# Gated linear attention and an SSM block on one core: blocks of 32 steps with a carried state, computed in small tiles of the TensorE array

## The chip, the core and the metric

The program runs on one core of a Trainium2 chip. A core has TensorE (a 128 x 128 multiply array that reads SBUF and writes PSUM), VectorE, ScalarE and GpSimd, each with its own in-order stream of instructions, and SyncE, which here only issues DMAs. The engines meet through semaphores. The metric is the device time of one execution in microseconds (us); lower is better. In the profile PE is TensorE's matmul side and PEld its weight loads, DVE is VectorE, ACT is ScalarE, POOL is GpSimd, SP is SyncE.

## The reference

Four batch entries, eight heads, 768 steps, 48 channels a head, all in float32. First a gated linear attention, a recurrence over the steps:

```python
for t in range(S):
    state = alpha[:, :, t, :, None] * state + einsum('bhd,bhe->bhde', k[:, :, t], v[:, :, t])
    y[:, :, t] = einsum('bhd,bhde->bhe', q[:, :, t], state)
```

The heads are then put side by side, x of shape (4, 768, 384), and go through a gated SSM block:

```python
val, gate = split(x @ w_in)              # 512 and 512 features
h = a * h + val[:, t]; ys[:, t] = h      # for each step, a = exp(A_log)
out = (silu(gate) * ys) @ w_out          # back to 384
```

## The kernel before

The sequence of a batch entry is cut into groups of G = 2 chunks of C = 128 steps, so there are 12 groups, three to a batch entry. A group goes through two routines: `attention(n)`, then `ssm(n)`. Both are Python generators; the loop at the end of the kernel runs them turn by turn, so that the pieces of `ssm(n-1)` stand between the levels of `attention(n)`. The tile framework under the kernel then sets the semaphores, and moves an instruction ahead of others of its engine where its own model of the times says so; the lists of instructions below are the order that results.

`attention(n)`, lines 167 to 285. Heads go in pairs, a pair filling the 128 partitions as 2 x 64 channels (48 and 16 of padding).

- Lines 178 to 188 transpose alpha, q and k to channels by steps on PE (`tp`, one PSUM buffer, `ps_tp`) and copy them to `T`, `Q` and `K`.
- Inside a chunk the pairs of steps s < t are dealt with by a binary tree of seven levels, l = 1 to 64. At each level ACT copies the odd blocks of `Q` into `Qz`, block-diagonal by the two heads of a pair (line 207, twice a level); PE computes the scores `sc` of a level with eight matmuls of 128 x 128 by 128 columns (line 218; line 215 for l = 32 and 64, where only the blocks are computed); DVE copies those that belong to the level into `A` through a mask (line 228; ACT at line 225 for l of 16 and more); and the running products grow by one doubling, `Q` on DVE (236), `K` and the block products `T` on POOL (237, 240). The next level's scores need the grown `Q` and `K`.
- For each of the two chunks: the output `y` from `A` and the values (252) and, behind the first chunk, from `Q` and the state `S_bd` (256); then the state of the next chunk, from a transpose of `K` (264), its copy `Kn` (266), the product `s1` with the values (270), the decay (276, 277) and two copies that make it block-diagonal (280).

`ssm(n)`, lines 287 to 323: transposes of x (292), the projection `pj` (302), the scan over the steps on DVE (305), the sigmoid on ACT and two products (310 to 312), the output product `o` (318) and its store. `w_in` and `w_out` come as float64 bits and are converted by eight DVE instructions for each of ten pieces (lines 110 to 121), during the first group.

In the profile a float32 matmul is two records, each a weight load on PEld and a matmul on PE, while a transpose is one: line 218's 480 matmuls are x960. "Record" below means one such pair.

Of the kernel before, what the change touches and what calls it, by code (L numbers as in the profile page):

```python
# [9 lines left out]
FP32 = mybir.dt.float32  # L10
# [7 lines left out]
def kernel(  # L18
# [10 lines left out]
):  # L29
    """Gated linear attention in chunks of C steps, then the gated SSM block, all in float32.  # L30

    Inside a chunk the pair (s < t) is weighted by prod(alpha[s+1..t]) per key channel.  The pairs
    are split by a binary tree: at level l, t lies in an odd block of l steps and s in the even
    block before it, so that the weight is (product from the block's start to t) times (product
    from s to its block's end).  Both are running products of alpha alone, grown level by level
    with the block totals: no logarithm, no division, nothing that overflows by the split.  After
    the last level they are the factors that join the chunk to the state that is carried.
    """
    nc = tc.nc
    B, H, S, D = q.shape  # L40
    DM = H * D                    # 384
    DI = moe_A_log.shape[0]       # 512
    C = 128                       # steps of a chunk
    G = 2                         # chunks of a group
    GC = G * C                    # tokens of a group
    NG = S // GC                  # groups of a batch entry
    NP = H // 2                   # pairs of heads; a pair fills the partitions as 2 x 64
# [4 lines left out]
    LEVELS = [1, 2, 4, 8, 16, 32, 64]  # L52
    ON_ACT = (16, 32, 64)         # blocks that start on partition quadrants: plain copies
    BY_BLOCK = (32, 64)           # products of the blocks alone
# [7 lines left out]
    p3 = pool("p3", 3)  # L62
    wst = pool("wst", 2)
    ps_sc = pool("ps_sc", 2, space=PS)
    ps_tp = pool("ps_tp", 1, space=PS)
    ps_mm = pool("ps_mm", 3, space=PS)

# [1 line left out]
    NBUF = 3  # L69
    pads = [{n: const.tile([C, G, H, DP], FP32, name=f"{n}_pad{i}") for n in "qka"} for i in range(NBUF)]  # L70
# [3 lines left out]
    vs = {}  # L74

    def load(n):
        b, g = divmod(n, NG)
        t = pads[n % NBUF]
        vs[n] = p3.tile([C, G, H, D], FP32, name="v_sb")
        for c in range(G):  # L80
            rows = ds(g * GC + c * C, C)
            for dst, src in ((t["a"][:, c, :, 0:D], alpha), (t["q"][:, c, :, 0:D], q),
                             (t["k"][:, c, :, 0:D], k), (vs[n][:, c], v)):
                nc.sync.dma_start(out=dst, in_=src[b, :, rows, :].rearrange("h p d -> p h d"))

    load(0)
    load(1)

# [6 lines left out]
    nc.sync.dma_start(out=a_log, in_=moe_A_log.rearrange("(a p) -> p a", p=C))  # L95
    nc.scalar.activation(a_dec, a_log, AF.Exp)

    # The weights come as the bits of float64, low word first: to float32, rounded to nearest.
# [3 lines left out]
    def load_weight(dst, src):  # L102
# [6 lines left out]
        # sign and exponent: the float32 +-2^e, with zero and infinity beyond its range  # L109
# [6 lines left out]
        # mantissa: 21 bits of the high word and the low word as their fraction  # L116
# [7 lines left out]
    def load_weights():  # L124
        for kk in range(NK):
            for i in range(2):
                load_weight(w_in[:, kk, ds(i * DI, DI)], moe_w_in[ds(kk * C, C), ds(i * DI, DI)])
                yield
        for cc in range(NI):
            load_weight(w_out[:, cc, :], moe_w_out[ds(cc * C, C), :])  # L130
            yield

    # at level l, column (r, j) of an odd block r takes the rows s of the even block r
    masks = {}
    for l in LEVELS:
        if l in ON_ACT:
            continue
        nb = C // (2 * l)
        mf = p2.tile([C, nb, l], FP32, tag="mask_f", name="mask_f")
        nc.gpsimd.memset(mf, 1.0)  # L140
        nc.gpsimd.affine_select(out=mf, in_=mf, compare_op=ALU.is_ge, fill=0.0, base=0,
                                channel_multiplier=1, pattern=[[-2 * l, nb], [0, l]])
        nc.gpsimd.affine_select(out=mf, in_=mf, compare_op=ALU.is_ge, fill=0.0, base=l - 1,
                                channel_multiplier=-1, pattern=[[2 * l, nb], [0, l]])
        m = const.tile([C, 2 * GP, C // 2], U8, name=f"mask{l}")
        nc.vector.tensor_copy(out=m, in_=mf.rearrange("p b l -> p (b l)")[:, None, :]
                              .to_broadcast([C, 2 * GP, C // 2]))
        masks[l] = m

    # weights of the pairs (s, t): [s, chunk, head, t]; s >= t stays zero  # L150
    As = [const.tile([C, G, H, C], FP32, name=f"A{i}") for i in range(2)]
    # the odd blocks of Q for the products, block-diagonal by the heads of a pair
    Qzs = [const.tile([C, GP, 2, C // 2], FP32, name=f"Qz{i}") for i in range(3)]
    for t in As + Qzs:
        nc.gpsimd.memset(t, 0.0)
    n_qz = 0
    # the state by pairs of heads, block-diagonal
    S_bds = [const.tile([C, NP, 2, D], FP32, name=f"S_bd{i}") for i in range(2)]
    for t in S_bds:
        nc.gpsimd.memset(t, 0.0)  # L160
    S_f = const.tile([C, NP, D], FP32, name="S_f")

    prev_h = [None] * NI

    xs = {}

    def attention(n):
        nonlocal n_qz
        b, g = divmod(n, NG)
        pad, v_sb = pads[n % NBUF], vs.pop(n)  # L170
        A = As[n % 2]

        # channels to the partitions: aT, qT * aT, kT as [(head of pair, channel), chunk, pair, step]
        T = p3.tile([C, 2 * GP * C], FP32, name="T")
        Q = p3.tile([C, G, NP, C], FP32, name="Q")
        K = p3.tile([C, G, NP, C], FP32, name="K")
        aT = T[:, 0:GP * C].rearrange("p (g j t) -> p g j t", g=G, j=NP)
        for name in "aqk":
            for c in range(G):
# [5 lines left out]
                elif name == "q":  # L185
                    nc.vector.tensor_mul(Q[:, c], tp, aT[:, c])  # L186
                else:
                    nc.scalar.activation(K[:, c], tp, AF.Copy)  # L188

        # the pairs s == t, whose weight is one  # L190
        qk = p2.tile([C, G, H, D], FP32, name="qk")
        dg = p2.tile([C, G, H], FP32, name="dg")
        nc.gpsimd.tensor_mul(qk, pad["q"][:, :, :, 0:D], pad["k"][:, :, :, 0:D])
        nc.vector.tensor_reduce(out=dg, in_=qk, axis=mybir.AxisListType.X, op=ALU.add)
        nc.gpsimd.tensor_mul(qk, v_sb, dg[:, :, :, None].to_broadcast([C, G, H, D]))

        # the pairs s < t, level by level
# [48 lines left out]
        for c in range(G):  # L246
# [13 lines left out]
            if last:  # L260
                continue
# [101 lines left out]
```

## Time and profile before

| | |
|---|---|
| median of 2 runs | 668.98 us (667.76 to 670.2) |
| span of the profiled execution, first to last instruction | 655.2 us |
| so, between the span and the runs' times | 12.6 to 15.0 us, 13.8 to the median |
| instructions recorded | 9150 |
| mean granted TensorE clock | 0.893 |
| DMA traffic | 28.91 MB, mean 44 GB/s |

The profile gives no time for its own execution other than the span; what lies around the span is taken as the 13.8 us to the median. Busy times of engines overlap, and a busy PE is not a full array: the records say that a matmul is in flight. The line of the granted clock, in tenths, tells how fast the array was allowed to run. A number in brackets behind a row of the timeline is how long the engine stood idle before it, and what ended that.

### The profile page before, as it was taken

The page shows a single profiled execution, that of the slowest core. Times are in us where ns is not written, and L with a number is a line of the kernel's source. Part 1 is how long each engine was busy: PE and PEld are TensorE (multiplying, and loading weights), DVE is VectorE, ACT ScalarE, POOL GpSimd, SP SyncE. Part 2 cuts the span into 40 slices and gives each one's busy share as a digit, 9 for nine tenths or more (in the row PEclk, how much of TensorE's full clock was granted, in tenths as well). Part 3 has the DMA queues.
Part 4 walks back from the last instruction along what each step waited for, and adds up shares of the span by engine and source line. Part 5 has one row for each costly group of instructions (what it writes and reads, how often), then busy time and mean ns, then how long its engine had stood idle before and what let it go on. Part 6 is the DMA issues. An engine that isn't in the chain of part 4 may idle for free.

```text
span 655.2 us, 9150 instructions
## 1 busy us (share of the span) xinstructions
PE 526.7 (80%) x3608; PEld 440.1 (67%) x3608; DVE 297.1 (45%) x392; ACT 235.5 (36%) x419; POOL 255.5 (39%) x330
## 2 busy tenths in 40 slices
PE   2657159969979978978968968968968968978987
PEld 1546149758768758758757758758758757867775
DVE  4676976138138138127227227226327326315512
ACT  1351034344334334334334334325325325315411
POOL 9732643253243253253343253352342352322411
PEclk9995559979979979979979979988989988987999
DMA  9935520050040050040040040032010000000000
GB/s 158 205 60 124 149 52 2 25 98 0 25 98 1 25 97 2 25 92 5 25 93 5 25 81 16 14 73 36 13 37 1 14 12 2 13 13 1 1 26 25
DMA packets 105307, 28.91 MB, mean 44 GB/s; under 512 B 100912, under 2 KB 103984, under 8 KB 105264
## 3 DMA queue, kind: packets, MB, share of 16 engines
q1 hardware_dynamic: 105264, 28.32, 21.9%
q8 instruction: 29, 0.48, 0.3%
q14 instruction: 14, 0.11, 0.1%
HBM read 23.60 MB, written 4.72 MB: 43 GB/s over the span
## 4 chain that ended last, share of the span: by engine, by line
PE 62%; POOL 11%; issue 10%; ACT 8%; DVE 7%; DMA 1%; POOLq 0%; DVEq 0%; SPq 0%; ACTq 0%
PE sc L218 17%; PE pj L302 11%; PE o L318 10%; POOL K L237 7%; PE y L252 7%; PE tp L182 6%; PE sc L215 5%; ACT Qz L207 3%; DVE Q L186 2%; PE y L256 2%; PE s L270 2%; ACT Kn L266 2%; PE tpk L264 2%; ACT K L188 1%; ACT T L184 1%
## 5 line engine op out<-in xcount | busy, mean ns | idle before, releaser
L218 PE MATMUL sc<-Qz,K 128*128 128x128 f32 x960 | 142.5, 308 | 26.4 <-POOL K L237 25.8
L237 POOL TENSOR_TENSOR K<-K,T 128x512 f32<-128x512 f32 x84 | 99.1, 1180 | 160.0 <-PE sc L218 91.6
L218 PEld LDWEIGHTS sc<-Qz,K 128*128 128x128 f32 x960 | 135.9, 222 | 35.8 <-POOL K L237 33.8
L207 ACT ACTIVATE Qz<-Q 64x512 f32<-64x512 f32 x168 | 107.3, 639 | 136.1 <-DVE Q L186 71.8
L302 PE MATMUL pj<-xT,w_in 128*128 128x256 f32 x576 | 132.3, 381 | 0.6 <-ACT xT L293 0.6
L302 PEld LDWEIGHTS pj<-xT,w_in 128*128 128x128 f32 x576 | 106.5, 191 | 13.3 <-ACT xT L293 0.8
L228 DVE COPY_PREDICATED A<-mask,sc 128x1024 f32<-128x1024 uint8 x48 | 89.6, 1867 | 31.1 <-PE sc L218 30.9
L236 DVE TENSOR_TENSOR Q<-Q,T 128x512 f32<-128x512 f32 x84 | 70.3, 837 | 54.0 <-ACT Qz L207 52.6
L312 POOL TENSOR_TENSOR f<-sg,hh 128x256 f32<-128x256 f32 x48 | 35.0, 730 | 107.6 <-DVE sg L311 98.9
L258 DVE TENSOR_TENSOR x_sb<-y,qk 128x384 f32<-128x384 f32 x24 | 13.4, 557 | 131.3 <-PE y L256 105.6
L318 PE MATMUL o<-w_out,f 128*128 128x384 f32 x192 | 69.2, 504 | 0.6 <-POOL f L312 0.6
L225 ACT ACTIVATE A<-sc 16x256 f32<-16x256 f32 (+2 forms) x84 | 44.1, 525 | 25.1 <-PE sc L215 18.1
L318 PEld LDWEIGHTS o<-w_out,f 128*128 128x128 f32 x192 | 33.7, 189 | 25.1 <-POOL f L312 6.0
L182 PE MATMUL tp<-ident,k_pad 128*128 128x128 f32 x96 | 26.8, 435 | 29.3 <-DVE Q L186 18.5
L252 PEld LDWEIGHTS y<-v_sb,A 128*128 128x128 f32 x384 | 47.8, 200 | 3.6
L182 PE MATMUL tp<-ident,q_pad 128*128 128x128 f32 x96 | 23.9, 392 | 32.3 <-issue 13.4
L280 POOL COPY S_bd<-S_f 64x192 f32<-64x192 f32 x40 | 19.1, 477 | 76.4 <-DVE S_f L277 58.5
L252 PE MATMUL y<-v_sb,A 128*128 128x48 f32 x384 | 48.7, 282 | 0.0
L310 ACT ACTIVATE sg<-pj 128x256 f32<-128x256 f32 x48 | 18.4, 383 | 77.1 <-DVE hh L305 76.9
L240 POOL TENSOR_TENSOR T<-T 128x512 f32<-128x512 f32 (+6 forms) x84 | 36.9, 440 | 19.6 <-ACT T L184 14.3
L182 PEld LDWEIGHTS tp<-ident,k_pad 128*128 128x128 f32 x96 | 17.2, 217 | 38.7 <-DVE Q L186 23.2
L182 PEld LDWEIGHTS tp<-ident,q_pad 128*128 128x128 f32 x96 | 15.0, 193 | 39.3 <-DVE Q L186 14.2
(57 smaller groups left out, 490.9 us busy)
## 6 DMA issues: line engine op xcount, KB each, us to landing
a_pad<-in_alpha_dram SPq DMA_DIRECT2D x24, 192.0 KB, 3.8
q_pad<-in_q_dram SPq DMA_DIRECT2D x24, 192.0 KB, 3.8
k_pad<-in_k_dram SPq DMA_DIRECT2D x24, 192.0 KB, 3.1
v_sb<-in_v_dram SPq DMA_DIRECT2D x24, 192.0 KB, 3.5
out_dram<-o_sb SPq DMA_DIRECT2D x24, 192.0 KB, 1.9
bits<-in_moe_w_in_dram SPq DMA_DIRECT2D x6, 512.0 KB, 5.2
bits<-in_moe_w_out_dram SPq DMA_DIRECT2D x4, 384.0 KB, 3.0
a_log<-in_moe_A_log_dram SPq DMA_DIRECT2D x1, 2.0 KB, 4.3
```

Of the source, the lines that this page charges most:

```text
L182: nc.tensor.transpose(tp[:, j, :], pad[name][:, c, 2 * j:2 * j + 2, :], ident)
L207: nc.scalar.activation(Qz[r, :, i, :].rearrange("p x (b l) -> p x b l", l=l), Qv[r, :, 1, :].rearrange("p (x b) l -> p x b l", b=nb), AF.Copy)
L218: nc.tensor.matmul(sc[:, c, j], K[:, c, j, :], Qz[:, c * NP + j], start=True, stop=True)
L225: nc.scalar.activation(A_b[ds(s0, l), :, ds(s0 + l, l)], sc_b[ds(s0, l), :, ds(r * l, l)], AF.Copy)
L228: nc.vector.copy_predicated(out=A.rearrange("p g h (b two l) -> p (g h b) two l", two=2, l=l)[:, :, 1, :], mask=masks[l].rearrange("p a (b ...
L236: nc.vector.tensor_mul(Qv[:, :, 1, :], Qv[:, :, 1, :], Tv[:, :, 0:1].to_broadcast([C, n2, l]))
L237: nc.gpsimd.tensor_mul(Kv[:, :, 0, :], Kv[:, :, 0, :], Tv[:, :, 1:2].to_broadcast([C, n2, l]))
L240: nc.gpsimd.tensor_mul(Tn, Tv[:, :, 0], Tv[:, :, 1])
L252: nc.tensor.matmul(y[:, h, :], A[:, c, h, :], v_sb[:, c, h, :], start=(h == 0), stop=(first and h == H - 1), skip_group_check=True)
L302: nc.tensor.matmul(pj[:, i, :], w_in[:, kk, ds(i * DI + cc * C, C)], xT[:, kk, :], start=(kk == 0), stop=(kk == NK - 1))
L312: nc.gpsimd.tensor_mul(f[:, cc, :], sg, hh)
L318: nc.tensor.matmul(o, f[:, cc, ds(c * C, C)], w_out[:, cc, :], start=(cc == 0), stop=(cc == NI - 1))
```

## The change

The tree stops at blocks of R = 32 steps: five levels, l = 1 to 16. A state is carried from block to block, eight blocks to a group, instead of from chunk to chunk. Every product of the attention is cut to small tiles of the array, each with its own rows (the channels of one head of the pair, or 32 of the steps) and its own 32 columns:

- scores: per level 64 matmuls of 64 rows by 32 columns, 16 columns moving, straight from strided views of `Q` (no `Qz`, no copies on ACT); the two heads go to two PSUM banks;
- states: `K` is transposed in 32 x 32 squares by one DVE instruction (`Kt`), then 128 matmuls of 32 by 32, 48 moving, in four pieces of 32 (`z`); the carried state `S_n` grows block by block, a product on POOL and a sum on DVE for each of eight blocks;
- outputs: 64 matmuls of 32 by 32 from `A` and the values, 64 of 64 by 32 from `Q` and the states.

`v` is loaded a second time in another layout, `v4`, by 16 DMAs a group. `A` shrinks from 2048 to 512 elements a partition. The masks are made on POOL alone. `attention` is split into four generators and a fixed loop interleaves `levels(n)`, `states(n-1)`, `transposes(n+1)`, `ssm(n-2)` and `outputs(n-1)`: three groups in flight, two more turns of the loop than groups. The scores have one PSUM buffer of two banks instead of two; the input pads have two buffers instead of three. `w_in` is converted value half first.

The diff's core, with the comments that it drops left out:

```diff
-    LEVELS = [1, 2, 4, 8, 16, 32, 64]
+    LEVELS = [1, 2, 4, 8, 16]
...
-    ps_sc = pool("ps_sc", 2, space=PS)
+    ps_sc = pool("ps_sc", 1, space=PS)
     ps_tp = pool("ps_tp", 1, space=PS)
-    ps_mm = pool("ps_mm", 3, space=PS)
+    ps_y = pool("ps_y", 1, space=PS)
+    ps_z = pool("ps_z", 1, space=PS)
+    ps_mm = pool("ps_mm", 2, space=PS)
...
+        v4s[n] = p3.tile([C, GR, NP, D], FP32, name="v4")
+        vv = v[b].rearrange("(j i) s d -> i j s d", i=2)
+        for qd in range(4):
+            for j in range(NP):
+                nc.sync.dma_start(
+                    out=v4s[n][ds(R * qd, R), :, j, :],
+                    in_=vv[qd // 2, j, ds(g * GC, GC), :].rearrange("(r s) d -> s r d", s=R))
...
+    def make_masks():
+        for l in LEVELS:
+            nb = R // (2 * l)
+            mf = p2.tile([C, NR, nb, l], FP32, tag="mask_f", name="mask_f")
+            nc.gpsimd.memset(mf, 1.0)
+            for qd in range(NR):
+                sl = mf[:, qd]
+                nc.gpsimd.affine_select(out=sl, in_=sl, compare_op=ALU.is_ge, fill=0.0, base=-R * qd,
+                                        channel_multiplier=1, pattern=[[-2 * l, nb], [0, l]])
+                nc.gpsimd.affine_select(out=sl, in_=sl, compare_op=ALU.is_ge, fill=0.0, base=R * qd + l - 1,
+                                        channel_multiplier=-1, pattern=[[2 * l, nb], [0, l]])
...
+    def levels(n):
...
+            sc = ps_sc.tile([C, 2, 512], FP32, tag="sc", name="sc")
+            scv = sc[:, :, 0:GP * R // 2].rearrange("p i (x b l) -> p i x b l", x=GP, l=l)
+            for c in range(G):
+                for j in range(NP):
+                    for r in range(NR):
+                        for i in range(2):
+                            rows, steps = ds(DP * i, DP), ds(R * r, R)
+                            nc.tensor.matmul(scv[steps, i, c * NP + j], K[rows, c, j, steps],
+                                             Qr[rows, c, j, r, :, 1, :], start=True, stop=True,
+                                             skip_group_check=True)
...
+    def states(n):
...
+        nc.vector.transpose(out=Kt.rearrange("p x d -> p (x d)"), in_=K.rearrange("p g j t -> p (g j t)"))
...
+            for r in (r2, r2 + 1):
+                g, rr = divmod(r, NR)
+                for j in range(NP):
+                    for qd in range(4):
+                        rows = ds(R * qd, R)
+                        nc.tensor.matmul(zv[rows, r - r2, j, :], Kt[rows, (g * NP + j) * NR + rr, :],
+                                         v4[rows, r, j, :], start=True, stop=True, skip_group_check=True)
...
+                    nc.gpsimd.tensor_mul(dS, S_n[:, r], Tb[:, g, :, rr:rr + 1].to_broadcast([C, NP, D]))
+                    nc.vector.tensor_add(dst, dS, zv[:, r - r2])
...
+    for n in range(N + 2):
+        if n + 2 < N:
+            load(n + 2)
+        if n + 1 < N:
+            load_v(n + 1)
...
+        for p in range(5):
+            step(lv)
+            if n == 0:
+                step(weights)
+                step(weights)
+            if p < 4:
+                step(sa)
+            step(tr)
+            if p < 4:
+                step(sm)
```

The order of PE, in a turn in the middle of the program. Before, one level of scores (eight matmuls) stands between two pieces of the projection, and the transposes of the next group follow in one stretch at the end; `x8` is eight matmuls.

```order
L218 MATMUL sc<-Qz_151,K 128x128 x8
L302 MATMUL pj<-xT,w_in 128x256 x6
L215 MATMUL sc<-Qz_149,K 32x2x32 x16
L318 MATMUL o<-w_out,f 128x384 x4
L215 MATMUL sc<-Qz_150,K 64x128 x8
L318 MATMUL o<-w_out,f 128x384 x4
L252 MATMUL y<-v_sb,A_148 128x48 x8
L256 MATMUL y<-S_bd_157,Q 128x96 x4
L264 MATMUL tpk<-ident,K 128x128 x4
L270 MATMUL s_778<-v_sb,Kn 64x48 x8
```

Here the outputs and the state of one chunk follow each other, before those of the second.

Now, the last two of the five steps of a turn and what follows them (`z` are the states, `tpx` the transposes of x):

```order
L226 MATMUL sc<-Q,K 32x16 x64
L274 MATMUL z<-v_797,Kt 32x48 x32
L195 MATMUL tp<-ident,q_pad_86 128x128 x4
L339 MATMUL pj<-xT,w_in 128x256 x6
L226 MATMUL sc<-Q,K 32x16 x64
L195 MATMUL tp<-ident,k_pad_87 128x128 x4
L299 MATMUL y<-v_sb,A_106 32x48 x64
L309 MATMUL y<-S_n,Q 32x48 x64
L195 MATMUL tp<-ident,k_pad_87 128x128 x4
L355 MATMUL o<-w_out,f 128x384 x4
L324 MATMUL tpx<-ident,x_sb 128x128 x3
L355 MATMUL o<-w_out,f 128x384 x4
```

The transposes, which stood together, are now spread singly between other work. A level's scores are 64 small matmuls in place of 8, a group's states 128 in place of 16 and 8 transposes, its outputs 128 in place of 24.

The order of DVE at the start, where the weights are converted. Before, the first piece follows the growth of the first group's `Q`:

```order
L228 COPY_PREDICATED A_147<-mask_145,sc 128x128x8
L236 TENSOR_TENSOR Q<-Q,T 128x32x16
L236 TENSOR_TENSOR Q<-Q,T 128x16x32
L110 TENSOR_SCALAR ex<-bits 128x512
L117 TENSOR_SCALAR w_in<-bits 128x512
```

Only the doubling for l = 64 is left of the first group's levels when the conversion begins.

Now it follows four levels of the third group:

```order
L243 COPY_PREDICATED A_106<-mask_177,sc 128x64x4
L235 TENSOR_TENSOR Q<-Q,T 128x64x8
L243 COPY_PREDICATED A_106<-mask_192,sc 128x32x8
L284 TENSOR_TENSOR S_n<-dS,z 128x192 x2
L126 TENSOR_SCALAR ex<-bits 128x512
L133 TENSOR_SCALAR w_in<-bits 128x512
```

The conversion moved behind two whole groups of levels on DVE, and the last of the third group's levels stands behind all ten pieces.

264 lines of the change are left out of this document (141 added, 123 removed).

## The prediction

> **What bounds the kernel now.** I read the page first (busy shares, slices, the chain), then the middle of the program in order of time, then the busy times by stretch, then the groups by line.
>
> ```profile
> PE 526.7 (80%) x3608; PEld 440.1 (67%) x3608; DVE 297.1 (45%) x392; ACT 235.5 (36%) x419; POOL 255.5 (39%) x330
> PEclk9995559979979979979979979988989988987999
> PE 62%; POOL 11%; issue 10%; ACT 8%; DVE 7%; DMA 1%; POOLq 0%; DVEq 0%; SPq 0%; ACTq 0%
> ```
>
> PE is the bound, and no other engine is above half; but the chain is PE for only 62%, and the granted clock dips once a group. One group in the middle shows where:
>
> ```profile
> 314.13 2.76 PE L302 MATMUL pj<-xT,w_in 128*128 128x256 f32 x12
> 316.82 1.09 PE L215 MATMUL sc<-Qz,K 128*32 128x64 f32 x32
> 317.84 2.94 PE L318 MATMUL o<-w_out,f 128*128 128x384 f32 x8
> 320.70 1.96 PE L215 MATMUL sc<-Qz,K 128*64 128x128 f32 x16
> 325.28 1.88 PE L252 MATMUL y<-v_sb,A 128*128 128x48 f32 x16
> 329.21 0.67 PE L270 MATMUL s<-v_sb,Kn 128*64 128x48 f32 x16 [0.69 <-ACT Kn L266]
> 333.81 0.66 PE L182 MATMUL tp<-ident,a_pad 128*128 128x128 f32 x4 [0.69 <-ACT T L184]
> 337.09 1.12 PE L182 MATMUL tp<-ident,q_pad 128*128 128x128 f32 x4 [1.27 <-DVE Q L186]
> 344.67 0.49 PE L292 MATMUL tpx<-ident,x_sb 128*128 128x128 f32 x3
> ...
> 0.00:57.90 57.90, 31.21 (x208) 27.25 (x208) 38.60 (x51) 17.70 (x29) 33.25 (x52) 0.93 0.93 139
> 57.90:135.90 78.00, 51.72 (x339) 43.09 (x339) 43.90 (x80) 21.50 (x38) 34.27 (x32) 0.72 0.23 60
> 184.00:234.30 50.30, 42.97 (x302) 35.79 (x302) 21.56 (x27) 19.58 (x35) 20.30 (x25) 0.90 0.17 37
> 584.80:635.00 50.20, 43.15 (x292) 36.08 (x292) 20.06 (x24) 19.37 (x35) 15.17 (x22) 0.90 0.03 9
> 635.00:655.20 20.20, 16.06 (x64) 12.02 (x64) 4.69 (x8) 2.51 (x6) 2.89 (x4) 0.98 0.06 20
> ```
>
> Projection and scores are back to back; from 329 on the transposes wait for their one PSUM buffer, and the same four take 0.66 us and then 1.12, because the clock has been lowered. The last rows are stretches (length; busy PE, PEld, DVE, ACT, POOL; clock; DMA share; GB/s). They cut the program into a start of 135.9 us, nine groups of (584.8 - 135.9) / 9 = 49.9, and an end of 70.4. In a group PE is busy for 43 and waits for 7.
>
> **The small matmuls: the price on which all hangs.** Removed a group are the large products (the last row, a copy of the transposes, is for the turn below):
>
> ```profile
> L218 PE MATMUL sc<-Qz,K 128*128 128x128 f32 x960 | 142.5, 308 | 26.4 <-POOL K L237 25.8
> L215 PE MATMUL sc<-Qz,K 128*64 128x128 f32 x192 | 23.5, 276 | 2.0 <-ACT Qz L207 2.0
> L215 PE MATMUL sc<-Qz,K 128*32 128x64 f32 x384 | 13.1, 221 | 1.6 <-POOL K L237 1.6
> L252 PE MATMUL y<-v_sb,A 128*128 128x48 f32 x384 | 48.7, 282 | 0.0
> L256 PE MATMUL y<-S_bd,Q 128*128 128x96 f32 x160 | 22.1, 283 | 1.9 <-POOL S_bd L280 1.9
> L270 PE MATMUL s<-v_sb,Kn 128*64 128x48 f32 x320 | 14.3, 235 | 12.4 <-ACT Kn L266 12.4
> L264 PE MATMUL tpk<-ident,K 128*128 128x128 f32 x80 | 13.9, 284 | 1.5 <-POOL K L237 1.5
> L184 ACT ACTIVATE T<-tp 128x512 f32<-128x512 f32 x24 | 14.3, 597 | 38.4 <-PE tp L182 38.4
> ```
>
> That is (142.5 + 23.5 + 13.1 + 48.7 + 22.1 + 14.3 + 13.9) / 12 = 23.2 us a group. In their place come 320 + 128 + 128 = 576 small matmuls, 1152 records. At s ns from one record to the next they cost 1.152 s us a group, and are no cheaper than what they replace from s = 20.1 on.
>
> No row has a tile of 64 or 32 rows, so s is bounded from both sides. Above: L215's 32-column form. The median record lasts 220 ns, so (1090 - 220) / 31 = 28 ns lie from one to the next, with 64 columns moving. Its 64-column form takes (1960 - 272) / 15 = 113 ns with 128 moving, 0.88 ns a column, so 64 columns last 56 ns: two records, in two column tiles, must run at once. Below: by the same 0.88 ns, 48 columns in four tiles at once give 10.6 ns and 16 columns in eight give 1.8; weights of 32 columns, at L252's (1880 - 282) / 15 = 107 ns for 128, last 27 ns, in four to eight tiles 3 to 7. So the array alone would allow about 7. Between stands what the sequencer can issue:
>
> ```profile
> L215 PE MATMUL sc<-Qz,K x576: 218/220/324, 42.2 to 622.7; 128*32 128x64 f32 x132, 128*64 128x128 f32 x60
> L182 PEldq EVENT_SEMAPHORE  x2: 51/51/51, 282.7 to 282.8; - x2
> ```
>
> The second row is two waits of PE's own sequencer, 125 ns apart unrounded; the first holds it for 51. Between them in the program stand four transposes, eight instructions. So eight go through in 74 ns, 9.3 each, and a record (load and matmul) in 18.6. It is the nearest row to a long stream of small instructions, and in a turn of this kernel 2304 of them come: I take s = 18.6, and keep 7 and 28 as ends.
>
> [...]
>
> **A turn of the new loop on PE.** Small matmuls 1.152 x 18.6 = 21.4 us. Kept work at full clock: transposes 6 x 0.66 = 4.0, `tpx` 2 x 0.49 = 1.0, projection 4 x 2.6 = 10.4 (its 2.76 less the overlap with the next row), output product 2 x 2.85 = 5.7. Sum 42.5. A change between large and small tiles costs 0.1: L215 begins 2.69 us after the projection ahead of it, which takes 2.6; some 22 changes a turn are 2.2. What else it waits for is hidden by the new order: the transposes now stand singly, with 3 to 6 us of other work between two that share the buffer, against 0.6 for its copy. Left over, two round trips of 0.69: 1.3. Turn: 46.0 us, against 49.9. So PE has nearly as much to do as before; what goes is 7 us of waits and slowed transposes, and what comes is tile changes.
>
> **The engines beside it.**
>
> ```profile
> L207 ACT ACTIVATE Qz<-Q 64x512 f32<-64x512 f32 x168 | 107.3, 639 | 136.1 <-DVE Q L186 71.8 <-DVE Q L236 55.1 <-PE sc L218 5.4
> L237 POOL TENSOR_TENSOR K<-K,T 128x512 f32<-128x512 f32 x84 | 99.1, 1180 | 160.0 <-PE sc L218 91.6 <-PE sc L215 59.1 <-ACT Qz L207 9.3
> L228 DVE COPY_PREDICATED A<-mask,sc 128x1024 f32<-128x1024 uint8 x48 | 89.6, 1867 | 31.1 <-PE sc L218 30.9
> L276 POOL TENSOR_TENSOR S_f<-S_f,T 128x192 f32<-128x192 f32 x16 | 14.1, 881 | 1.3
> L277 DVE TENSOR_TENSOR S_f<-S_f,s 128x192 f32<-128x192 f32 x16 | 5.7, 354 | 17.7 <-PE s L270 17.7
> GB/s 158 205 60 124 149 52 2 25 98 0 25 98 1 25 97 2 25 92 5 25 93 5 25 81 16 14 73 36 13 37 1 14 12 2 13 13 1 1 26 25
> ```
>
> ACT loses line 207 (8.9 us a group) and the copies of `A` and `Kn`: off the path, nothing gained directly. POOL: five `K` products for seven, -2.4, but eight decays of 0.88 for one or two, +5.7: about 22 of 46, hidden. DVE: masked copies of 256 for 1024 elements, five at 0.35 (row 277) to 0.47 (a quarter of 1867) for four, -5; two doublings less; eight sums of 0.35, +2.5; the 32 x 32 transpose of `Kt` is in no row, by the nearest of 1024 elements 0.35 to 1.9: about 19 of 46, hidden. The states are a chain, eight times 0.88 + 0.35 and some 0.2 of signals, 11.4 us; in four pieces a turn apart by 7, covered. SP issues 16 more DMAs a group; `v` a second time is 0.39 MB twice over, 0.79 MB, and at the 98 GB/s of a loading slice 8 us of a turn: hidden.
>
> **Start and end.** Masks are now 40 small selects on POOL, and `K` of the first group must wait behind them. The rows of the start:
>
> ```profile
> 6.46 1.07 POOL L143 TENSOR_SCALAR_AFFINE_SELECT mask_f<-mask_f 128x64 f32<-128x64 f32 x2
> 26.85 3.47 PE L218 MATMUL sc<-Qz,K 128*128 128x128 f32 x16 [1.70 <-POOL K L237]
> 41.15 1.33 DVE L110 TENSOR_SCALAR ex<-bits 128x512 uint32<-128x512 uint32 x1
> 65.75 0.43 DVE L110 TENSOR_SCALAR ex<-bits 128x512 uint32<-128x512 uint32 x1 [6.63 <-DMA bits<-in_moe_w_in_dram]
> 87.10 0.55 DVE L121 SCALAR_TENSOR_TENSOR w_out<-w_out,ex 128x384 f32<-128x384 f32 x1
> ```
>
> A select took 0.5 with 64 elements; with 16 I take half, 10 us for 40, and reach the first `K` product at 27 (before, 25). Levels with nothing between them go scores (2.4) then `K` (1.2) and two signals: 3.8, or 19 a group. Three groups, the second held up by its transposes and by decays on POOL, bring DVE to the weights at about 93. Ten pieces took from 41.2 to 87.6, of which 6.6 was a wait for their DMA and some 5 other work: 35, with the sums and scans between them 41, so the third turn ends at 134. Nine full turns follow; then one without levels (states and outputs 9.5, `ssm` 17, transposes and changes 3, = 29.3) and a last `ssm` alone as in the last stretch, 20.2.
>
> 134 + 9 x 46.0 + 29.3 + 20.2 = 597.5 us of span, and with the 13.8 around it **611 us**, against 669. Each ns of s is worth 1.152 x 9 = 10.4 in the full turns, 1.8 in the fourteen bare levels and 0.2 at the end: 12.4 us.
>
> **Rivals.** (1) *PE issues or loads no faster than the fastest row*, 28 ns: 611 + 9.4 x 12.4 = 728, slower. It decides from s = 24.4. For it: no row is faster, and 2304 instructions a turn are far more than ever stood in one burst. Against: that row is full of moving columns, and the sequencer's row. (2) *The tiles overlap better and the sequencer runs ahead*, s = 12: 529. For it: the 74 ns may hold the end of a wait. [...] (3) *One buffer for the scores*: the next level waits for the masked copy and for `K`, as in the start's row (1.70), if the work between is shorter than I think: 5 x 9 x 1.4 = 63, so 674. Against: 4.5 us of other work stand between two levels. (4) *The clock gate* takes a stream of small tiles for idleness: at half clock the 21 us of large work a turn take twice as long, 800 us. For it: the dips follow idle stretches, not long ones; against: PE is never idle here.
>
> **Chances.** Forecast (s from 15 to 22) 0.42; rival 1 0.21; rival 2 0.20; rival 3 0.12; rival 4 0.05. A measurement of this kernel tells about 2%, 13 us, from no change. The forecast and rival 2 are faster: 0.62. Rival 3 lies at the edge, 0.08 within 2% and 0.04 above; with rivals 1 and 4 slower is 0.30. The range of 8 in 10 reaches into rivals 1 and 2, s from 13.3 to 27.4: 545 to 720. The forecast's own range is 566 to 653.
>
> **What would show it.** Right: full turns of about 46 us in which PE is hardly idle; the scores' x128 records (64 matmuls) in about 2.4 us; no dips of the clock; transposes of 0.66; POOL and DVE under half busy; the first projection not before the weights, at about 105. Wrong: x128 in 3.5 us (rival 1) or 1.6 (rival 2); scores behind idle time that a masked copy or `K` ends (3); a clock of 5 in slices in which PE is full (4); a third turn that ends later than 145.

## The result, and the profile after

The changed kernel takes 620.4 us, the median of two runs (618.36 and 622.45), against 668.98 before: a ratio of 0.930, with a 95% interval of 0.917 to 0.942. The forecast was 611, and the time lies in its range. Its span is 616.7 us, so only 1.7 us lie around it (618.36 is the same execution).

From the page of the changed kernel: busy shares, the granted clock in 40 slices, the queue that carries instructions (packets, MB, share), and the chain that ended last.

```profile
PE 474.8 (77%) x14888; PEld 373.1 (61%) x14888; DVE 242.6 (39%) x464; ACT 70.9 (11%) x147; POOL 272.3 (44%) x358
PEclk9997675858879979987888888888988888887999
q8 instruction: 117, 1.92, 1.3%
PE 69%; issue 16%; DVE 7%; POOL 4%; DMA 1%; SPq 1%; ACT 0%; POOLq 0%; DVEq 0%; ACTq 0%
```

PE is still the bound, but two things are new. "issue" is 16% of the chain, where it was 10%, and in the turns it now marks times in which PE itself stood idle though nothing in the profile held it. And the clock, which before dipped once a group, is at 0.8 in most slices of the turns. One step of a turn without such an idle time, and the next one with it (start, length; in brackets the idle time before the row):

```profile
250.37 1.26 PE L226 MATMUL sc<-Q,K 64*32 64x16 f32 x128
251.56 0.88 PE L274 MATMUL z<-v,Kt 32*32 32x48 f32 x64
252.37 0.66 PE L195 MATMUL tp<-ident,a_pad 128*128 128x128 f32 x4
252.86 2.76 PE L339 MATMUL pj<-xT,w_in 128*128 128x256 f32 x12
255.55 1.26 PE L226 MATMUL sc<-Q,K 64*32 64x16 f32 x128
256.74 0.61 PE L274 MATMUL z<-v,Kt 32*32 32x48 f32 x34
260.01 0.54 PE L274 MATMUL z<-v,Kt 32*32 32x48 f32 x30 [2.66 <-issue]
260.48 0.82 PE L195 MATMUL tp<-ident,a_pad 128*128 128x128 f32 x4
261.09 4.31 PE L339 MATMUL pj<-xT,w_in 128*128 128x256 f32 x12
265.33 1.26 PE L226 MATMUL sc<-Q,K 64*32 64x16 f32 x128
```

The small matmuls are far cheaper than forecast: 128 records of scores in 1.26 us, of which the last record is some 0.2, so about 8 ns from one to the next where 18.6 was taken. The first step takes 255.55 - 250.37 = 5.18 us. The second takes 9.78: PE stands still for 2.66 us in the middle of 32 equal matmuls (64 records) with no wait on record, and the projection behind it, at a lowered clock, takes 4.31 us for 2.76.

The outputs of a turn show what the stops have in common:

```profile
192.24 1.29 PE L299 MATMUL y<-v_sb,A 32*32 32x48 f32 x100
195.14 0.53 PE L299 MATMUL y<-v_sb,A 32*32 32x48 f32 x28 [1.61 <-issue]
195.60 1.12 PE L309 MATMUL y<-S_n,Q 64*32 64x48 f32 x100
198.60 0.39 PE L309 MATMUL y<-S_n,Q 64*32 64x48 f32 x28 [1.87 <-issue]
```

From one stop to the next there are 28 + 100 = 128 records, which are 256 instructions. On the page above, PE's 14888 records over 117 instruction packets are 127 to a packet of 1.92 MB / 117 = 16 KB; in the kernel before, 3608 records went with 29 packets. In the unrounded trace every stop put down to issue in the turns lies at such a boundary. So TensorE's program comes in pages of 256 instructions, and PE waits for a page. When pages follow each other without pause, between 50 and 100 us, their packets start 3.8 us apart (median), and never less than 3.3 anywhere. Before the change a page lasted 655 / 29 = 23 us, its packets were never less than 17 us apart, and none of PE's longer idle times in the nine groups stood at issue.

The stretches of the program (length; busy PE, PEld, DVE, ACT, POOL; clock; DMA share; GB/s): the levels of three groups, the weights, nine turns, the end.

```profile
0.00:104.00 104.00, 58.40 (x2639) 46.58 (x2639) 29.71 (x51) 9.53 (x16) 58.68 (x117) 0.80 0.46 76
104.00:157.10 53.10, 37.27 (x460) 25.99 (x461) 48.72 (x103) 6.02 (x11) 25.01 (x19) 0.71 0.67 141
157.10:570.60 413.50, 339.43 (x11145) 270.37 (x11143) 151.28 (x285) 48.64 (x104) 179.34 (x207) 0.87 0.29 56
570.60:616.70 46.10, 39.74 (x649) 30.17 (x647) 12.94 (x26) 6.67 (x16) 9.27 (x15) 0.99 0.07 23
```

And PE's longer waits in the nine turns (total, times, longest):

```profile
PE z L274 <- issue: 38.0, 17, 3.3
PE y L309 <- issue: 16.4, 8, 2.4
PE y L299 <- issue: 11.9, 9, 1.6
PE sc L226 <- issue: 3.2, 3, 1.6
PE z L274 <- DVE A L243: 1.6, 1, 1.6
```

A turn is 413.5 / 9 = 45.9 us, 46.0 in the forecast. With the shorter rows the waits for pages are 72.4 us in 40 stops, 8.0 a turn. The one wait put down to another engine (1.6 us, the last row) lies at a boundary of pages too, so it may be a forty-first. By its rows a turn without stops and at full clock would be four steps of 5.18 and a fifth of about 11, some 32 us. The remaining 45.9 - 8.0 - 0.2 - 32, some 6 us, go to the lowered clock. The trace bears that out: its records of the granted clock have only two values, full and half, and the half stands for 105.8 us of the nine turns, 7.0 of them idle. Half of the other 98.8 is 5.5 us a turn.

### The profile page after: what moved, and what is told of

Same layout as the page of the kernel before. It is cut to its first block, busy times and chain, and to the rows that moved or that the text cites. A ratio compares the mean times of both kernels' runs of the same rounds, so it can differ in the third digit from the quotient of the medians.

```text
span 616.7 us, 31643 instructions
## 1 busy us (share of the span) xinstructions
PE 474.8 (77%) x14888; PEld 373.1 (61%) x14888; DVE 242.6 (39%) x464; ACT 70.9 (11%) x147; POOL 272.3 (44%) x358
## 3 DMA queue, kind: packets, MB, share of 16 engines
q8 instruction: 117, 1.92, 1.3%
## 4 chain that ended last, share of the span: by engine, by line
PE 69%; issue 16%; DVE 7%; POOL 4%; DMA 1%; SPq 1%; ACT 0%; POOLq 0%; DVEq 0%; ACTq 0%
PE pj L339 23%; PE sc L226 12%; PE o L355 12%; PE tp L195 8%; PE z L274 8%; PE y L299 3%; PE y L309 3%; POOL K L236 2%; PE tpx L324 1%; DMA k_pad<-in_k_dram 1%; DVE w_in L137 1%; DVE ex L126 1%; DVE ex L130 1%; DVE w_in L133 1%; DVE w_in L136 1%
## 5 line engine op out<-in xcount | busy, mean ns | idle before, releaser
L339 PE MATMUL pj<-xT,w_in 128*128 128x256 f32 x576 | 165.1, 445 | 10.5 <-DVE sg L348 4.5
L339 PEld LDWEIGHTS pj<-xT,w_in 128*128 128x128 f32 x576 | 127.0, 229 | 33.1 <-DVE sg L348 5.1
L226 PE MATMUL sc<-Q,K 64*32 64x16 f32 x7680 | 82.8, 194 | 32.5 <-issue 19.2
L226 PEld LDWEIGHTS sc<-Q,K 64*32 64x32 f32 x7680 | 74.6, 113 | 51.5 <-issue 32.9
L274 PE MATMUL z<-v,Kt 32*32 32x48 f32 x3072 | 56.9, 219 | 47.4 <-issue 40.7
L274 PEld LDWEIGHTS z<-v,Kt 32*32 32x32 f32 x3072 | 45.4, 116 | 56.3 <-issue 51.1
L283 POOL TENSOR_TENSOR dS<-S_n,Tb 128x192 f32<-128x192 f32 x92 | 51.4, 558 | 63.5 <-DVE S_n L284 62.1
L235 DVE TENSOR_TENSOR Q<-Q,T 128x512 f32<-128x512 f32 x60 | 41.5, 691 | 92.8 <-PE sc L226 92.6
L284 DVE TENSOR_TENSOR S_n<-dS,z 128x192 f32<-128x192 f32 x92 | 32.6, 354 | 80.4 <-PE z L274 47.8
L309 PE MATMUL y<-S_n,Q 64*32 64x48 f32 x1472 | 21.4, 226 | 19.2 <-issue 17.9
L241 POOL TENSOR_TENSOR T<-T 128x512 f32<-128x512 f32 (+3 forms) x48 | 29.9, 622 | 9.0 <-ACT T L197 7.1
L243 DVE COPY_PREDICATED A<-mask,sc 128x256 f32<-128x256 uint8 x60 | 32.8, 547 | 0.0
```

What stands on the lines that cost most here:

```text
L226: nc.tensor.matmul(scv[steps, i, c * NP + j], K[rows, c, j, steps], Qr[rows, c, j, r, :, 1, :], start=True, stop=True, skip_group_check=True)
L235: nc.vector.tensor_mul(Qv[:, :, 1, :], Qv[:, :, 1, :], Tv[:, :, 0:1].to_broadcast([C, n2, l]))
L243: nc.vector.copy_predicated(out=A.rearrange("p i x (b two l) -> p i (x b) two l", two=2, l=l)[:, :, :, 1, :], mask=masks[l].rearrange("p ( ...
L274: nc.tensor.matmul(zv[rows, r - r2, j, :], Kt[rows, (g * NP + j) * NR + rr, :], v4[rows, r, j, :], start=True, stop=True, skip_group_check ...
L283: nc.gpsimd.tensor_mul(dS, S_n[:, r], Tb[:, g, :, rr:rr + 1].to_broadcast([C, NP, D]))
L309: nc.tensor.matmul(yv[steps, i, c, j, :], Q[rows, c, j, steps], S_n[rows, c * NR + r, j, :], start=False, stop=(c == G - 1 and j == NP - 1 ...
```

## The experiments

Theory S (supply) was formed from these rows; theory A (array) holds that small matmuls cost what the array and the sequencer take for them. Nine runs, one of them the kernel before once more, tell them apart and measure the other terms.

### Every score matmul twice

```diff
-                            nc.tensor.matmul(scv[steps, i, c * NP + j], K[rows, c, j, steps], ...)
+                            for _ in range(2):
+                                nc.tensor.matmul(scv[steps, i, c * NP + j], K[rows, c, j, steps], ...)
```

> Every score matmul is issued twice, with the same operands and the same target (the result is unchanged): 64 more small matmuls a level, 320 a group, 1280 instructions of TensorE. Theory S (supply): TensorE's program reaches it in pages of 256 instructions, one page about every 3.8 us at best, and the idle times put down to 'issue' are waits for a page. Five more pages a turn: a full turn grows by 11 us (if all of it is bound by supply, 15 pages at 3.8 = 57 us against 46) to 20 us (5 pages at 3.9), the time to 750 to 860 us, and the number of idle times put down to issue grows by about 4 to 5 a turn. Theory A (array): small matmuls only cost what they take in a burst, 1.26 us for 128 records; 640 more records a turn are 6 us, and the time goes to about 690 us with no more idle times than now.

It took 845.5 us. From its page, the busy shares and the instruction packets:

```profile
PE 620.6 (74%) x22568; PEld 509.6 (60%) x22568; DVE 248.7 (29%) x464; ACT 70.9 (8%) x147; POOL 268.8 (32%) x358
q8 instruction: 177, 2.90, 1.5%
```

Its nine turns in the view by stretch (columns as above):

```profile
196.20:797.70 601.50, 456.23 (x16905) 376.74 (x16903) 154.65 (x284) 48.64 (x105) 180.43 (x205) 0.78 0.19 39
```

A turn is 601.5 / 9 = 66.8 us, 20.9 more, just over the upper end of theory S; theory A had 6. There are 79 stops for 40, as long as before (145.2 / 79 = 1.84 us against 1.81), again 127 records to a packet (22568 / 177), and the clock is lower. 66.8 us for the 14.7 pages of a turn (16905 / 9 / 128) are 4.6 us a page.

### The same instructions, small among large

```diff
+            for x in range(4):
+                go(lv, 2)        # 16 scores
+                go(sm)           # one 128 x 256 matmul of the projection
...
+        for x in range(4):
+            go(ou)               # 16 matmuls of the outputs
+            go(sm)               # one of the output product
```

> The same instructions in another order: in the full turns 16 scores, then one pair of 128 x 256 projection matmuls, then 16 scores and so on; states in eights between projection matmuls and transposes; 16 output matmuls, then one matmul of the output product, and so on. Theory S: a page of 256 instructions then holds several us of large work, the idle times put down to issue become fewer and shorter (below 1 us), the dips of the granted clock that follow them go, and a full turn comes to the supply of 10 pages at 3.8 = 38 us, 36 to 41, against 46.0; the time to 535 to 575 us. Theory A: the idle times come from the small matmuls themselves and stay, and some 40 more changes of the tile size at 0.1 us add 4 us a turn: about 655 us.

It took 593.8 us: better than the changed kernel, but slower than the 535 to 575 us of theory S, and far from the 655 of theory A. The nine turns in the view by stretch:

```profile
159.60:541.40 381.80, 364.34 (x11107) 226.67 (x11105) 156.60 (x285) 49.73 (x104) 181.19 (x207) 0.98 0.32 61
```

And a piece of one in order of time:

```profile
173.57 0.39 PE L226 MATMUL sc<-Q,K 64*32 64x16 f32 x32
173.89 0.70 PE L346 MATMUL pj<-xT,w_in 128*128 128x256 f32 x2
174.52 0.34 PE L226 MATMUL sc<-Q,K 64*32 64x16 f32 x32
174.79 0.70 PE L346 MATMUL pj<-xT,w_in 128*128 128x256 f32 x2
175.42 0.34 PE L226 MATMUL sc<-Q,K 64*32 64x16 f32 x32
```

The stops fell to 17 in nine turns, 15.5 us in all, and the clock is 0.98: with hardly any stops it is not lowered, though the matmuls are the same. In the unrounded trace it is halved just twice, behind the two longest stops (2.0 and 1.8 us); behind the others, of at most 1.3 us, it stays full. That much is as theory S said. But a turn is 42.4 us, because PE is busy for 40.5 of it in place of some 32. The cycle of 32 records of scores and one matmul of the projection (two records) takes 174.52 - 173.57 = 0.95 or 0.90 us, against 32 x 8.2 ns = 0.26 and 2.69 / 6 = 0.45 in long rows: 0.1 us for each change between small and large tiles, as forecast, but 59 more of them a turn (71 for 12) rather than forty, and some of those between outputs and output product cost 0.15.

### The weights earlier

```diff
     load(1)
+    for _ in range(4):
+        next(weights)
...
+                if p == 1:
+                    load(2)
+                    load_v(1)
```

> The ten weight pieces are issued by SP ahead of the loads of the third group and of the second group's values, and four of them ahead of the first turn in the program, so that VectorE converts them between the levels of the first and second group. Theory: VectorE is busy for 33 us of the first 107, so the 41 us of conversion that now stand alone between 104 and 145 us find room there; the third turn, which now ends at 157.3 us, ends between 112 and 130, and the time falls by 27 to 45 us, to 575 to 592. Rival: the loads or the levels of the first groups are pushed back by what the conversion gains (the DMA engines are all busy for the first 25 us), the third turn ends at 145 to 157, and the time is 605 to 620.

It took 604.7 us, and the rival held: the third turn ended at 155.1 us, 2 us sooner. (The rest of the gain lies in the turns, 44.6 us each at a clock of 0.89 for 0.87. Nothing in this edit bears on them; the runs of the kernel before are up to 16 us apart as well.) The stretch of the conversion:

```profile
54.00:92.00 38.00, 8.70 (x464) 7.16 (x441) 38.00 (x73) 1.20 (x2) 23.14 (x12) 0.56 0.52 125
```

And from POOL's instructions in order of time, one product in it:

```profile
68.79 8.67 POOL L204 TENSOR_TENSOR qk<-q_pad,k_pad 128x768 f32<-128x768 f32 x1 [7.01 <-DMA k_pad<-in_k_dram]
```

DVE was busy for the whole 38 us and the levels of the second group hardly moved: PE was busy for 8.7. The same product takes 1.8 us where DVE does not convert.

### Square tiles, a third fewer instructions

```diff
-                    for r in range(NR):
+                    for r in range(2):
                         for i in range(2):
-                            rows, steps = ds(DP * i, DP), ds(R * r, R)
+                            rows, steps = ds(DP * i, DP), ds(64 * r, 64)
                             nc.tensor.matmul(scv[steps, i, c * NP + j], K[rows, c, j, steps], ...)
...
-    As = [const.tile([C, 2, GP, R], FP32, name=f"A{i}") for i in range(2)]
+    As = [const.tile([C, 2, GP, 64], FP32, name=f"A{i}") for i in range(2)]
...
-                    for r in range(NR):
-                        rows = ds(R * r, R)
+                    for r in range(2):
+                        rows = ds(64 * r, 64)
                         nc.tensor.matmul(yv[rows, i, c, j, :], A[rows, i, c * NP + j, :], ...)
```

> Scores and the product of A and the values in tiles of 64 rows by 64 columns (two blocks of 32 steps at once; the mask keeps what lies in one block): 32 matmuls a level for 64, with 32 columns moving for 16, and 32 for 64 in the outputs; 384 small matmuls a group for 576, 7.4 pages of instructions a turn for 9.9. Theory S: 2.5 pages fewer; at 2.1 us of idle time and about 1 us of lowered clock for each idle time put down to issue, two to three of the 4.5 a turn go, and a full turn falls from 46.0 to 37 to 41 us; the time to 560 to 590 us (the fourteen bare levels of the start gain too). Theory A: what counts is columns loaded and moved, which are as many or twice as many for the same four to eight tiles; a turn stays within 2 us of 46, and the time within 600 to 640 us.

It took 494.8 us, 126 less than the changed kernel and well beyond what theory S had promised. Its instruction packets, from the page:

```profile
q8 instruction: 81, 1.33, 1.2%
```

Its nine turns in the view by stretch:

```profile
150.00:448.20 298.20, 287.40 (x7688) 235.53 (x7687) 172.84 (x285) 48.52 (x104) 177.94 (x206) 0.99 0.41 77
```

One step in order of time:

```profile
150.20 1.14 PE L224 MATMUL sc<-Q,K 64*64 64x32 f32 x64
151.26 0.88 PE L272 MATMUL z<-v,Kt 32*32 32x48 f32 x64
152.07 0.66 PE L193 MATMUL tp<-ident,a_pad 128*128 128x128 f32 x4
152.57 2.75 PE L337 MATMUL pj<-xT,w_in 128*128 128x256 f32 x12
155.25 1.13 PE L224 MATMUL sc<-Q,K 64*64 64x32 f32 x64
```

The array takes as long as ever, 5.05 us for this step against 5.18, so theory A is out. But the step now has 288 instructions, and a page of 256 lasts 4.5 us, longer than the 3.8 us in which the next one comes. The stops fall to 8 in nine turns, the clock is 0.99, and a turn is 298.2 / 9 = 33.1 us. What the expectation had too small was the effect: it took away two or three stops of 4.5, and nearly all went.

### The kernel before, once more

No edit.

> The kernel before, unchanged, so that the time and the span of one and the same execution stand side by side. In the changed kernel's runs 1.7 to 2 us lie around the span. Theory: it is the same here, and the 13.8 us that the prediction took for it was the difference of two executions: with a time of 655 to 670 the span is 2 us less. Rival: 12 to 15 us lie around the span of this kernel.

The first line of its page:

```profile
span 656.9 us, 9150 instructions
```

Its time was 658.66 us, 1.8 more than its span. So nothing like 13.8 us lies around a span; the 668.98 and the profile of 655.2 were different executions, and fourteen more runs of the kernel before, beside this and the kernels below, took from 656.9 to 673.3 us.

### No conversion

```diff
-        nc.vector.tensor_scalar(out=ex, in0=hi, scalar1=20, scalar2=0x7FF,
-                                op0=ALU.logical_shift_right, op1=ALU.bitwise_and)
...
+        nc.vector.tensor_scalar(out=mh, in0=hi, scalar1=0x3FFFFFFF, scalar2=None, op0=ALU.bitwise_and)
```

> The eight VectorE instructions that convert a weight piece are replaced by one, which copies the upper words (the weights are then wrong; left out is the conversion). Theory C (the conversion stands alone at the end of the start, and while VectorE runs it GpSimd's products take two to eight times as long): without it the third turn ends at 115 to 128 us in place of 157.3, GpSimd's products of 128 x 512 last 1.1 to 1.6 us in the start and the block sums' products 0.5, none 3 or more, and the time falls to 578 to 592. Rival: the third turn is held by levels, pages and states; it ends after 140 and the time stays above 600.

It took 603.1 us, as the rival had it. The third turn ended at 138.1 us, between the two expectations: 19 us of the start hang on the conversion, not 41, because the levels of three groups end no sooner (the first projection stands at 105 us, at 108 before) and the projection and outputs of the first group must still follow them. What theory C said of POOL held in the main. Two products of the changed kernel that ran beside the conversion, from POOL's instructions in order of time:

```profile
107.35 4.39 POOL L236 TENSOR_TENSOR K<-K,T 128x512 f32<-128x512 f32 x1 [2.52 <-PE sc L226]
131.68 3.18 POOL L283 TENSOR_TENSOR dS<-S_n,Tb 128x192 f32<-128x192 f32 x1 [3.17 <-DVE S_n L284]
```

Two of the same groups without the conversion, in the same view:

```profile
108.62 1.58 POOL L223 TENSOR_TENSOR K<-K,T 128x512 f32<-128x512 f32 x1 [0.38 <-PE sc L213]
114.77 0.51 POOL L270 TENSOR_TENSOR dS<-S_n,Tb 128x192 f32<-128x192 f32 x1 [3.92 <-DVE S_n L271]
```

Without the conversion POOL's products of these two shapes take at most 1.95 and 0.69 us up to the end of the third turn. Beside the conversion not every product is held up, and DVE is held up too. Here, in the changed kernel, it is DVE's instruction that waits, 2.03 us for the 0.41 of its like, while POOL's takes its usual time:

```profile
118.30 1.99 POOL L204 TENSOR_TENSOR qk<-q_pad,k_pad 128x768 f32<-128x768 f32 x1
118.54 2.03 DVE L133 TENSOR_SCALAR w_in<-bits 128x512 uint32<-128x512 uint32 x1
```

### The values' second layout loaded three times only

```diff
-        for qd in range(4):
+        for qd in range(4) if n < 3 else ():
             for j in range(NP):
                 nc.sync.dma_start(
```

> The second layout of the values (v4, 16 DMAs a group) is loaded for the first three groups alone and used again by the later ones (left out: the right values in the states from the fourth group on). Theory S: the idle times put down to issue have nothing to do with this traffic: about 55 of them, 90 to 100 us in all, and a time of 612 to 622. Rival: pages of instructions come late because the DMA engines carry the same data traffic: with 7 MB less the idle times shrink by a third or more, and the time falls below 595.

It took 606.4 us, between the two. The number that decides is that of the stops: 42 in nine turns, 68.6 us, 7.6 a turn against 8.0, and not a third less. The pages are late with this traffic or without it. Its nine turns in the view by stretch:

```profile
156.80:558.10 401.30, 330.61 (x11144) 265.90 (x11142) 151.70 (x285) 48.55 (x104) 179.23 (x207) 0.89 0.19 41
```

A turn is 401.3 / 9 = 44.6 us, 1.3 less: 0.4 of that are stops, and the rest goes with the clock, 0.89 for 0.87. Why the same stops lowered the clock less in this run is open.

### Both: square tiles and early weights

The edits of the two kernels above together.

> The square tiles of e4 with the early weights of e3. If the two gains add, 494.8 - 14 (what e3 gained over the changed kernel's span) = 481, 474 to 488. Rival: with the levels of the start shorter the conversion finds no room and holds GpSimd's products in the levels instead; no gain, 490 to 500.

It took 479.3 us (478.2 to 484.9 in four runs), 0.726 of the kernel before (0.716 to 0.735), the fastest of all. Start, nine turns and end in the view by stretch:

```profile
0.00:139.10 139.10, 81.87 (x2011) 66.20 (x2012) 82.08 (x153) 15.62 (x28) 88.31 (x111) 0.84 0.62 114
139.10:432.80 293.70, 283.69 (x7688) 232.70 (x7687) 171.50 (x285) 48.43 (x104) 179.69 (x207) 1.00 0.39 76
432.80:477.70 44.90, 40.09 (x585) 30.66 (x583) 12.96 (x26) 6.67 (x16) 9.28 (x15) 0.99 0.07 24
```

And a row of POOL in the start, in order of time:

```profile
56.78 22.09 POOL L239 TENSOR_TENSOR T<-T 128x512 f32<-128x512 f32 x4 [3.61 <-ACT T L195]
```

The sum came out as expected, but not its reason: the start gained 11 us here (150.0 to 139.1) where it had gained 2. And POOL was held as in the third experiment: four products that take 2.6 us elsewhere took 22.

### A shorter conversion

```diff
+        nc.vector.tensor_scalar(out=ex, in0=hi, scalar1=0x07FFFFFF, scalar2=3,
+                                op0=ALU.bitwise_and, op1=ALU.logical_shift_left)
+        nc.vector.scalar_tensor_tensor(out=ex, in0=lo, scalar=29, in1=ex,
+                                       op0=ALU.logical_shift_right, op1=ALU.bitwise_or)
+        nc.vector.scalar_tensor_tensor(out=mh, in0=hi, scalar=0x80000000, in1=ex,
+                                       op0=ALU.bitwise_and, op1=ALU.bitwise_or)
```

> e8 with three VectorE instructions a weight piece in place of eight (shifts and masks alone, right for weights below 2 in magnitude, as these are; the low 29 bits are cut off, which float32 values widened to float64 have at zero). Theory C: in e6 the start lost 19 us with the conversion gone, in e8 the third turn still ends at 139 us; with 5/8 of the conversion gone some 8 to 16 us more go from the start, the turns stay at 33, and the time is 463 to 471 us. Rival: in e8 the conversion is already hidden and the start is set by levels and loads: 475 to 482.

It took 486.6 us (480.5 to 489.4), no gain over the kernel above and longer than either expectation. In its profile the start did shorten by 10.6 us, as theory C had it, and the next turns gave it back. Its start and the three turns behind it, by stretch:

```profile
0.00:128.50 128.50, 93.40 (x2012) 73.50 (x2012) 70.47 (x103) 15.91 (x28) 72.70 (x111) 0.87 0.68 119
128.50:248.00 119.50, 109.52 (x2573) 87.18 (x2571) 60.88 (x96) 16.71 (x36) 61.07 (x71) 0.91 0.44 77
```

Three turns of 39.8 us follow, at a clock of 0.91, where the other kernel has 33 at 1.00. In the program the framework has now put the projection of these turns ahead of the states, which then stand together near the end of the turn. That this order is the cause was not tried, and the profiled execution, 489.4 us, is the longest of the four, so that part of the 20 us may be its own.

## Why the number was right and the way to it was not

The sum of the prediction and what the profile has in its place: start 134, measured 157.1; nine turns of 46.0, 414, measured 413.5; the turn without levels and the last piece 49.5, measured 46.1; around the span 13.8, measured 1.7. That is 611 + 23.1 - 0.5 - 3.4 - 12.1 = 618. Three errors all but cancelled, and the term that came out to the tenth was itself a sum of two large errors: a turn has some 14 us less of work and tile changes than forecast, and 14 us of stops and lowered clock that were not in it. So the number was luck.

**The small matmuls.** The step that failed is "eight go through in 74 ns, 9.3 each, and a record (load and matmul) in 18.6". That price was taken for a long stream, from the one place at which the trace of before showed eight instructions pass, and those 74 ns may have held the end of a wait, as rival 2 said; no run tested that. In bursts a record takes 8 ns (scores) to 11 (states): by the rows of a turn, scores, states and outputs come to 5 x 1.19 + 4 x 0.81 + 2.7 = 11.9 us, with their tile changes, where 21.4 and some of the 2.2 for changes stood in the sum. So rival 2 was right about the array, with s below the 12 that it took, an estimate that no row showed (11.9 / 1.152 = 10.3), and wrong about the time, 529: what it had over was taken by something that no list held. Over 32 scores in a row the closest records are 5.2 ns apart (unrounded trace of the changed kernel, at 50.0 us for one). A price per record was the wrong form. The limit is one on instructions in a stretch of time, 256 in 3.8 us, and bursts of small matmuls run into it however evenly the average would fit.

**Waits and clock.** The forecast had 1.3 us of waits and no dips, and said that PE would hardly be idle. Measured a turn: 8.0 us of waits for pages and some 6 of lowered clock. The step that failed is "PE is never idle here", and with it the reasons against rival 4: that the clock dips after idle stretches was read rightly, but the change brought forty new idle stretches into the nine turns. In these kernels the clock follows the stops: with 8.0 us of them a turn it is 0.87, with 16.1 (the doubled scores) 0.78, with 1.7 (spread) 0.98, with 0.8 (square) 0.99. That the stops are pages is shown by their distance of 128 records, by the doubled scores and by the two kernels that take them away, one without removing an instruction. The count could have been read ahead of time: the page of before has a row for instruction packets, 29 of them, and the order of the new program shows 1152 small records a turn. How fast packets can follow each other it does not show: they were never less than 17 us apart there. In the trace of the changed kernel a packet is 16 KB (1.92 MB over 117), and one starts only when PE has gone into the page ahead of it (unrounded: at 227.7 us, for one, 1.5 us behind a stop that ended at 226.2); no more than one page comes ahead. The trace also splits the 3.8 us. At the stops of over 1 us the next packet starts 1.0 to 2.9 us (median 1.35) after PE has gone on, and PE goes on 2.2 to 2.9 us (median 2.5) after a packet has started, of which the packet itself takes 1.1. What fills the rest of both is open.

**Kept work.** Transposes 0.66, projection 2.69, output product 2.6 to 2.9, tile changes 0.1: as taken, wherever the clock is full. Of changes between small and large tiles a turn has 12, where 22 were taken. The transposes, spread singly, wait for their one buffer no more; the 1.3 us of round trips did not come at all.

**One buffer for the scores (rival 3).** In nine turns one wait, 1.6 us, is put down to a masked copy, and it lies at a boundary of pages. At the start PE waits for `K`, as before (13.0 us in six waits up to 157 us). For the turns the rival is out.

**The other engines.** DVE, POOL and ACT are busy for 17, 20 and 5 us a turn, about what was worked out for the first two (19 and 22), and hold nothing. SP's extra loads cost at most what the seventh experiment shows.

**The start.** Two steps failed in "bring DVE to the weights at about 93 ... so the third turn ends at 134". DVE reached them at 104: pages were late in the levels too (19.8 us of stops up to 157 us, 18.5 of them by then), and the clock was 0.80. How much of the delay each made was not separated. And the conversion took the 41 us of the forecast, 104 to 145, but the turn does not end with it: the output product needs the last pieces, and 12 us of projection, transposes and output product stood behind. Masks, the first `K` product (24 us for 27) and the first projection (108 us for 105) were about as forecast. The conversion itself is worth 19 us of the start, as the sixth experiment shows, and it can't simply be laid over the levels, because POOL's products, on which the levels wait, are held up while DVE converts (8.67 us for 1.8 in the third experiment, 22.09 for 2.6 in the eighth).

**Around the span.** Taking the difference of two executions for a cost was the error: the term is 1.7 us, and the kernel before varies by 16 us between runs.

## What to carry to other kernels

When a change multiplies an engine's instructions, count them by stretch of time, not only their total time: here PE needed 3.8 us of work in every 256 instructions, and each of four steps of a turn had 416 in 5.2 us. The cheapest remedy was not a better order but fewer, larger instructions: tiles of 64 by 64 left the array time of a step where it was and took 126 us off, while spreading them cost 0.1 to 0.15 us at each change of the tile size. And an idle time of two microseconds on PE is to be priced with what follows it: here 8 us of stops a turn brought some 6 more at a lowered clock.

## What the runs showed of the hardware that was not expected

- Records of 64 rows by 32 columns with 16 columns moving follow each other after 8 ns (128 records in 1.26 us, eight tiles), those of 64 by 64 with 32 moving after 14.5 (64 in 1.14), those of 32 by 32 with 48 moving on the diagonal tiles after 11.
- TensorE's instructions arrive in packets of 16 KB, 127 records each, 3.3 us apart at the closest. Behind most idle times of 1.6 to 3.3 us (24 of 28 in the nine turns, within 2 us) the clock was halved and the large matmuls took up to 1.6 times their length (4.31 us for 2.76), while behind single ones of 0.7 to 1.3 us in the spread kernel it was not (the projection's two records behind them took their 0.70). The length of one idle time is not all: in the kernel before, a row of them of 0.7 to 1.3 us was enough (the four transposes of 1.12 us for 0.66).
- While DVE runs the integer conversion, some products on POOL take three to eight times as long (8.67 us for 1.82, 4.39 for 1.58, 22.09 for 2.6), and some of DVE's own instructions are held up by POOL's (2.03 for 0.41). What decides which of them are held up no run here shows.
